# LSH attention, then a mixture of experts: first batch's x kept whole, its block sums in unit 4's first layer, the second batch's spread over units 5 to 7, attention's pace from 1300 to 2000

## The chip, the cores and the metric

The kernel runs on one core of a Trainium2 chip. The metric is the device time of one execution in microseconds (us); lower is better. The engines are TensorE (PE in the profile, with its weight loads as PEld), VectorE (DVE), ScalarE (ACT), GpSimd (POOL) and SyncE (SP), whose queue issues nearly all DMAs here.

## What is computed

```python
def _attn_ref(q, k, v, proj):        # q, k, v: 2 x 8 x 768 x 64; proj: 64 x 6
    q_bits = (np.einsum('bhsd,dk->bhsk', q, proj) > 0).astype(np.int64)
    ...
    mask = q_bucket[:, :, :, None] == k_bucket[:, :, None, :]
    scores = scale * np.matmul(q, k.transpose(0, 1, 3, 2))
    scores = np.where(mask, scores, -1000000000.0)
    scores = scores - np.max(scores, axis=-1, keepdims=True)
    attn = np.exp(scores)
    attn = attn / (np.sum(attn, axis=-1, keepdims=True) + 1e-09)
    return np.matmul(attn, v)

def _moe_ref(x, domain_probs, w1, w2):   # x: 1536 x 512; w1: 4 x 512 x 1024; w2: 4 x 1024 x 512
    p = domain_probs / (domain_probs.sum(-1, keepdims=True) + 1e-09)
    for e in range(E):
        h = np.maximum(x @ w1[e], 0.0)
        out += p[:, e:e + 1] * (h @ w2[e])
```

x is the attention's output, with the 8 heads side by side: 2 batches of 768 rows by 512 columns. All is float32.

## The kernel before

**Numbers.** A float32 product is made as three products of rounded parts: each operand is split into hi (ACT copies it into the rounded type) and lo (the operand minus hi, on POOL or DVE), and hi x hi, hi x lo and lo x hi are summed in PSUM.

**Attention.** Heads 0 to 7 belong to batch 0, heads 8 to 15 to batch 1. A head has six tiles of 128 rows. For each tile TensorE makes scores, DVE and ACT the exponentials. For heads 8 to 15 DVE turns blocks of 32 x 32 (`stage_x`, line 503, into `t`), three tiles to a group, and a DMA writes the group to DRAM (`scr`, line 509); four DMAs read it back in the wanted order into `pt` (`stage_y`, line 520). When both groups are there, TensorE makes the product with V in 24 matmuls (`stage_v`, line 538), DVE and ACT copy it out (`stage_u`, line 565), and POOL multiplies by the reciprocal of the row sums (`stage_m`). The pool `ptp` has three buffers for `pt`, `t` of the second group, and later for parts of w1. SP issues in order: the first reads of a head wait until the V product before has freed a buffer; then come the second group's write to `scr`, loads of the next head and of weights, and the second reads, which wait for that write to land.

For batch 0, `stage_m` writes x at once as hi and lo (tiles `xhi`, `xlo`), from a small tile `xf`, which then is free again. For batch 1 it leaves x whole in `xraw`.

**Experts.** The work on one batch is eight units (4 experts x 2 halves of 512 hidden columns), numbered 0 to 7 for batch 0 and 8 to 15 for batch 1. A unit is a first layer (x by w1, relu, split into `hh` and `hl`) and a second layer (by w2, six groups of rows, each added into `acc` by DVE, line 748). Units 0 to 4 are plain (`unit`): the first layer has eight groups of 12 matmuls of 384 columns. From unit 5 on (`FAST = 5`), `unit_fast` makes the first layer from seven products of blocks twice over instead of eight. These need sums of blocks of x, t1 = b12 - b11, t2 = b22 - t1, t4 = t2 - b21 and t3 = b22 - b12 (b11, b12 the left and right halves of x's first two row blocks, b21 and b22 of its last two), each split into hi and lo, and sums s1 to s4 of blocks of w1 (`split_w1_fast`). In the first product of a half, `pa` is copied out by ACT (`mt<-pa`, line 1060); the fourth product then adds into the same PSUM tile.

**Preparation before.** While a second layer runs, each of its six groups is followed by one step of the preparation of the next unit's w1. In unit 4's second layer the same groups are also followed by a step of `x_ops_first`: four adds on POOL rebuild x as hi + lo (line 882), and then each step makes one sum (DVE), its hi (ACT) and its lo (POOL or DVE). In unit 7's second layer the steps are those of `x_ops`, for batch 1: eight hi and lo pairs, five of them issued before the first group.

**Order.** The program is written out as one order by hand. Attention of batch 1 runs between the groups of batch 0's units: both are generators that yield their cost. After each yield of the experts (1960 for a first-layer group, 2600 for a second-layer group), the loop takes attention steps until their cost is level:

```python
n_att = sum(652 + ... for b, h, t in seq if b) + H * 1632 + (LAG_M[1] + 2) * DRAIN
...
    while da < dm * ATT_PACE * n_att / n_moe:
        x = next(att, None)
```

The steps after the last scores, in which the last heads are turned, read back and multiplied by V, cost `DRAIN` each. At the end of unit 4's first layer `drained()` issues what is left of attention.

Of the kernel before, what the change touches and what calls it, by code (L numbers as in the profile page):

```python
# [8 lines left out]
F32 = mybir.dt.float32  # L9
F32R = mybir.dt.float32r  # L10
ACTF = mybir.ActivationFunctionType
# [35 lines left out]
DRAIN = 1300  # L47
# [5 lines left out]
def tile_lsh_attention__then__domain_moe(  # L53
# [16 lines left out]
    KD = DM // P  # L70
    HALF = 512
# [20 lines left out]
    ptp = ctx.enter_context(tc.tile_pool(name="ptp", bufs=3))  # L92
# [8 lines left out]
    ps1 = ctx.enter_context(tc.tile_pool(name="ps1", bufs=4, space=PSUM))  # L101

# [300 lines left out]
    xf = {}  # L403
# [67 lines left out]
    def stage_t(b, h, t):  # L471
        pt, _ = probs_t.pop((b, h, t))
        g, o = divmod(t, G)
        if o == 0:
            if b or g == 0:
                t0 = ptp.tile([P, NT, GN], F32, tag="pt", name="pt")
                parts[b, h, g] = [t0[:, a : a + TW] for a in range(0, NT, TW)]
            else:
                parts[b, h, g] = [hp.tile([P, TW, GN], F32, tag=tag, name="pth") for tag in ("hh", "hl")]
            pts[b, h, g] = [x[:, c] for x in parts[b, h, g] for c in range(TW)]  # L480
        for i, a in enumerate(range(0, NT, TW)):
            ps = one("ptps")
            for c in range(TW):
                nc.tensor.transpose(ps[:, c * P : (c + 1) * P], pt[:, (a + c) * P : (a + c + 1) * P], ident)  # L484
            src = ps[:, : TW * P].rearrange("p (c n) -> p c n", c=TW)
            dst = parts[b, h, g][i][:, :, o * P : (o + 1) * P]
            if i and o % 2 == 0:
                nc.vector.tensor_copy(dst, src)
            else:
                nc.scalar.activation(dst, src, ACTF.Copy)  # L490
# [4 lines left out]
    def stage_x(b, h, t):  # L495
        g, o = divmod(t, G)
        if o == 0:
            pool, tag = (ptp, "pt") if g else (ex, "t1")
            turned[b, h, g] = pool.tile([P, G, S], F32, tag=tag, name="t1")
# [15 lines left out]
    def stage_y(b, h, g):  # L515
        scr = scrs.pop((b, h, g))
        pt = ptp.tile([P, NT, GN], F32, tag="pt", name="pt")
# [28 lines left out]

    def stage_u(b, h):
# [4 lines left out]
        for g in range(2):  # L552
            pts.pop((b, h, g))
            if b:
                x = xraw[:, j, g * GN : (g + 1) * GN]
            else:
                if not odd:
                    xf[b, j, g] = xs.tile([P, GN], F32, tag=f"xf{g}", name="xf", bufs=1)
                x = xf[b, j, g]
# [9 lines left out]
    def stage_m(b, h, g):  # L569
        j = h // 2  # L570
        sl = slice(g * GN, (g + 1) * GN)
        x = xraw[:, j, sl] if b else xf.pop((b, j, g))
# [166 lines left out]
    KH = KD // 2  # L739
# [18 lines left out]
    def second_layer(b, u, first_u, hs, w2, xo=None):  # L758
# [6 lines left out]
        for s in range(NS - 1, -1, -1) if blocks else range(NS):  # L765
            for t in range(TS):
# [23 lines left out]
                if xo is not None:  # L790
                    next(xo, 0)
# [3 lines left out]
        for _ in xo or ():  # L795
            pass
# [22 lines left out]
    def unit(b, u, first_u):  # L819
        w1hi, w1lo = wts[first_u + u, 0]  # L820
        sp2 = split_w(first_u + u, 1) if first_u + u else iter(())
        hs = {}
        for s in range(NS):
            sl = slice(s * SB, (s + 1) * SB)
            for f in range(FC):
# [14 lines left out]
                next(sp2, 0)  # L840
                yield 1960
# [31 lines left out]
    b11, b12 = xraw[:, 0:KH, 0:SB], xraw[:, 0:KH, SB:S]  # L873
    b21, b22 = xraw[:, KH:KD, 0:SB], xraw[:, KH:KD, SB:S]

    xrs = {}

    def x_ops_first():
        raw = ex.tile([P, 3, S], F32, tag="t1", name="xr")
        raws = [raw[:, j] for j in range(3)] + [ld.tile([P, S], F32, tag="tqk", name="xr3")]  # L880
# [4 lines left out]
        left, right = slice(0, SB), slice(SB, S)  # L885
        for n, j, sl in (("b11", 0, left), ("b21", KH, left), ("b22", KH, right)):
            xop[n] = tuple([x[0, j + kk][:, sl] for kk in range(KH)] for x in (xhi, xlo))
        pair_in("t1", ((xp, "xe0"),))
        pair_in("t2", ((xp, "xe1"),))
        t1 = combine(raw[:, 0:KH, right], raw[:, 0:KH, left], ALU.subtract)  # L890
        put_hi("t1", t1)
        put_lo("t1", t1, nc.gpsimd)
        yield

        def mixed_rows(f):
            t = pp.tile([P, KH, SB], F32, tag="p", name="xc")
# [12 lines left out]
        yield
        pair_in("t3", ((stk, "q1"), (stk, "al")))  # L910
        t3 = mixed_rows(lambda kk: dict(in0=raws[KH + kk][:, right], in1=raw[:, kk, right]))
        put_hi("t3", t3)
        put_lo("t3", t3, nc.vector)
        yield

    def x_ops():
        pair_in("b11", ((stk, "ah"), (stk, "k2")))
        pair_in("t1", ((stk, "ah"), (stk, "k2")))
        t1 = combine(b12, b11, ALU.subtract)
        put_hi("b11", b11)  # L920
# [12 lines left out]
        pair_in("b22", ((xp, "xe1"),))
# [80 lines left out]
    def unit_fast(b, u, first_u):  # L1014
# [151 lines left out]
```

## Time and profile before

| | |
|---|---|
| time, median of 3 runs (lowest to highest) | 733.28 us (730.88 to 734.75) |
| the profiled execution's own time | 732.77 us |
| its span | 730.7 us |
| PE busy | 709.9 us, 97% of the span |
| DVE busy | 512.3 us, 70% |
| ACT busy | 337.9 us, 46% |
| POOL busy | 319.6 us, 44% |
| granted clock, mean over the span | 0.988 |
| moved by DMA | 87.77 MB |

Busy is time in which an engine executes; the shares are means over stages with different limits. The granted clock is TensorE's, as a share of full speed. The span is what the profile covers, and 2.1 us of the execution's time lie outside it.

### The profile page before, as it was taken

What the parts mean: (1) busy time and instruction counts of PE and PEld (TensorE: products, weight loads), DVE (VectorE), ACT (ScalarE), POOL (GpSimd) and SP (SyncE); (2) the same over time, 40 slices, a digit from 0 to 9 for tenths busy, and PEclk for the clock granted to TensorE, in tenths of its full rate; (3) what the DMA queues carried; (4) which work ended last, traced back from release to release, by engine and by line L of the source; (5) the groups of instructions that cost most, each with busy time, mean ns of one, the idle gap of its engine ahead of it and who ended that gap; (6) DMA issues with size and microseconds to landing.
All of it is one profiled execution on the core that took longest, in us unless ns stands there. A gap on an engine that the chain in (4) does not pass through costs nothing.

```text
span 730.7 us, 10185 instructions
## 1 busy us (share of the span) xinstructions
PE 709.9 (97%) x3714; PEld 596.9 (82%) x3714; DVE 512.3 (70%) x806; ACT 337.9 (46%) x661; POOL 319.6 (44%) x289
## 2 busy tenths in 40 slices
PE   8999999999999999997979999899999999999998
PEld 6766766978878879875859989698988989899896
DVE  6898898858567657631597685987668576685863
ACT  6887887553553534512234343443434334353440
POOL 6358677524534534302654342753334242343420
PEclk9999999999999999998989999999999999999999
DMA  6323263988889869777011121142112221112202
GB/s 145 67 45 92 62 124 63 238 235 235 224 217 293 238 189 307 204 217 215 1 57 59 58 91 55 48 154 87 57 58 72 73 86 56 61 57 83 91 1 86
DMA packets 90849, 87.77 MB, mean 120 GB/s; under 512 B 53168, under 2 KB 55728, under 8 KB 90800
## 3 DMA queue, kind: packets, MB, share of 16 engines
q1 hardware_dynamic: 89776, 86.80, 42.8%
q8 instruction: 29, 0.48, 0.3%
q10 hardware_dynamic: 1024, 0.33, 0.2%
q14 instruction: 20, 0.16, 0.1%
HBM read 65.04 MB, written 22.07 MB: 119 GB/s over the span
## 4 chain that ended last, share of the span: by engine, by line
PE 79%; DVE 7%; DMA 6%; issue 3%; SPq 2%; POOL 1%; ACT 1%; POOLq 0%; DVEq 0%; ACTq 0%
PE mps L754 10%; PE mps L756 10%; PE mps L755 10%; PE pv L538 8%; DMA pt<-scr 3%; PE ptps L484 3%; PE sps L418 3%; PE sps L416 3%; PE mps L1026 3%; PE mps L1025 3%; PE mps L1022 3%; PE mps L801 3%; PE mps L803 3%; PE mps L802 3%; PE pa L1022 2%
## 5 line engine op out<-in xcount | busy, mean ns | idle before, releaser
L754 PE MATMUL mps<-w2hi,hh 128*128 128x512 f32 (+1 forms) x388 | 151.6, 391 | 3.2 <-DVE acc L748 3.2
L756 PE MATMUL mps<-w2hi,hl 128*128 128x512 f32 (+1 forms) x388 | 150.9, 389 | 0.0
L755 PE MATMUL mps<-w2lo,hh 128*128 128x512 f32 (+1 forms) x388 | 150.9, 389 | 0.0
L1008 POOL TENSOR_TENSOR w2lo<-ws,w2hi 128x512 fp32r<-128x512 f32 x44 | 56.0, 1297 | 145.6 <-ACT w2hi L1007 126.3
L423 DVE TENSOR_SCALAR_CACHE_REDUCE p<-sps 128x768 f32<-128x768 f32 x96 | 90.1, 940 | 20.9 <-PE sps L418 19.2
L748 DVE SCALAR_TENSOR_TENSOR acc<-mps,pe,acc 128x512 f32<-128x512 f32 (+1 forms) x85 | 62.9, 741 | 50.6 <-PE mps L756 49.4
L439 ACT ACTIVATE p<-p,nb 128x768 f32<-128x768 f32 x96 | 89.5, 932 | 18.7 <-DVE p L423 18.3
L754 PEld LDWEIGHTS mps<-w2hi,hh 128*128 128x128 f32 x388 | 73.2, 189 | 18.7 <-DVE acc L748 3.6
L756 PEld LDWEIGHTS mps<-w2hi,hl 128*128 128x128 f32 x388 | 73.2, 189 | 15.6
L755 PEld LDWEIGHTS mps<-w2lo,hh 128*128 128x128 f32 x388 | 73.3, 189 | 14.0
L538 PE MATMUL pv<-pt,tv 128*64 128x384 f32 x288 | 72.6, 516 | 4.8 <-DMA pt<-scr 4.7
L967 POOL TENSOR_TENSOR w1lo<-ws,w1hi 128x512 fp32r<-128x512 f32 x33 | 52.0, 1579 | 50.6 <-ACT w1hi L963 29.6
L1035 ACT ACTIVATE hh<-mt 128x384 fp32r<-128x384 f32 x66 | 34.7, 525 | 64.1 <-DVE mt L1080 40.8
L538 PEld LDWEIGHTS pv<-pt,tv 128*64 128x64 f32 x288 | 26.6, 143 | 40.7 <-issue 32.4
L835 ACT ACTIVATE hh<-mps 128x384 fp32r<-128x384 f32 x40 | 19.6, 489 | 79.7 <-PE mps L803 79.6
L503 DVE STREAM_TRANSPOSE t<-p 128x768 f32<-128x768 f32 x48 | 46.3, 964 | 12.1 <-ACT p L439 12.0
L416 PE MATMUL sps<-ah,q 128*128 128x384 f32 x192 | 53.9, 362 | 0.8 <-DVE p L423 0.8
L801 PE MATMUL mps<-xs,w1hi 128*128 128x384 f32 x160 | 54.1, 338 | 0.0
L803 PE MATMUL mps<-xs,w1lo 128*128 128x384 f32 x160 | 53.9, 337 | 0.0
L802 PE MATMUL mps<-xs,w1hi 128*128 128x384 f32 x160 | 53.8, 336 | 0.0
L233 POOL TENSOR_SCALAR q<-ah 64x768 fp32r<-64x768 f32 (+1 forms) x33 | 27.1, 822 | 59.2 <-ACT ah L345 44.9
L418 PE MATMUL sps<-k,al 76*128 76x384 f32 x192 | 49.9, 340 | 0.7 <-POOL k L233 0.3
(158 smaller groups left out, 1560.3 us busy)
## 6 DMA issues: line engine op xcount, KB each, us to landing
ws<-in_moe_w_dram SPq DMA_DIRECT2D x64, 512.0 KB, 3.9
scr<-t SPq DMA_DIRECT2D x16, 1152.0 KB, 8.5
pt<-scr SPq DMA_DIRECT2D x64, 288.0 KB, 6.0
tv<-in_v_dram SPq DMA_DIRECT2D x16, 192.0 KB, 5.2
tqk<-in_q_dram SPq DMA_DIRECT2D x30, 96.0 KB, 3.5
out_dram<-acc SPq DMA_DIRECT2D x11, 256.0 KB, 2.0
tqk<-in_k_dram SPq DMA_DIRECT2D x28, 96.0 KB, 3.5
rdb<-row SPq DMA_DIRECT2D x14, 192.0 KB, 6.1
```

What stands on the lines that cost most here:

```text
L416: nc.tensor.matmul(ps[:, i, :NH], q1[:, sl], k1[:, i * NH : (i + 1) * NH], start=True, stop=False)
L418: nc.tensor.matmul(ps[:, i, :NH], q2[0:MQE, sl], k2[0:MQE, i * NH : (i + 1) * NH], start=False, stop=True)
L423: nc.vector.tensor_scalar(out=two(pt), in0=ps[:, :, :NH], scalar1=MASKED, scalar2=MASKED, op0=ALU.min, op1=ALU.min, accum_out=nb,)
L439: nc.scalar.activation(pt, pt, ACTF.Exp, bias=nb, scale=-1.0, accum_out=dens[b, h, r][:, o : o + 1])
L538: nc.tensor.matmul(dst, vvs[b, h][:, c], pts[b, h, g][c], start=c == 0, stop=c == NT - 1, tile_position=(0, g * D),)
L748: nc.vector.scalar_tensor_tensor(out=acc, in0=ps, scalar=pcol, in1=acc, op0=ALU.mult, op1=ALU.add)
L754: nc.tensor.matmul(ps, hh[:, ts], w2hi[:, f, cs], start=n == 0, stop=False)
L755: nc.tensor.matmul(ps, hh[:, ts], w2lo[:, f, cs], start=False, stop=False)
L756: nc.tensor.matmul(ps, hl[:, ts], w2hi[:, f, cs], start=False, stop=n == FC - 1)
L801: nc.tensor.matmul(ps[:, :SB], w1hi[:, kk, fs], xhi[b, kk][:, sl], start=kk == 0, stop=False)
L802: nc.tensor.matmul(ps[:, :SB], w1hi[:, kk, fs], xlo[b, kk][:, sl], start=False, stop=False)
L803: nc.tensor.matmul(ps[:, :SB], w1lo[:, kk, fs], xhi[b, kk][:, sl], start=False, stop=kk == KD - 1)
```

## The change

The first batch's x is kept whole: `stage_u` and `stage_m` work in two tiles `xrs` (tags `xe0` and `xe1`) in place of the small `xf`, and the four adds that rebuilt x are gone. Its sums are made in unit 4's first layer, one step behind every other group of its eight; all lo parts are on POOL. They lie in the buffers of heads' q and k, so that they can stand only behind the last scores. For the second batch, `x_ops` is replaced by two generators: `x_ops_early` makes b11, t1 and t2 in unit 5's second layer and t4 and b21 in unit 6's, one step behind every other group, and `x_ops_late` makes b22 and t3 in unit 7's. `ptp` gets two buffers and a third under a tag of its own, which attention uses in the same turn of three as before. `DRAIN` goes from 1300 to 2000; the sum `n_att` of all attention costs thereby goes from 94080 to 102480.

```diff
-DRAIN = 1300
+DRAIN = 2000
...
-    ptp = ctx.enter_context(tc.tile_pool(name="ptp", bufs=3))
+    ptp = ctx.enter_context(tc.tile_pool(name="ptp", bufs=2))
...
+    def pt_tile(shape, name):
+        turn[0] += 1
+        if turn[0] % 3:
+            return ptp.tile(shape, F32, tag="pt", name=name)
+        return ptp.tile(shape, F32, tag="ptb", name=name, bufs=1)
...
-    xf = {}
+    xrs = [xp.tile([P, KH, S], F32, tag=f"xe{i}", name="xr") for i in range(KD // KH)]
...
+    def x_raw(b, j):
+        return xraw[:, j] if b else xrs[j // KH][:, j % KH]
...
-                if xo is not None:
+                if xo is not None and (nxt == NU or tt % 2):
                     next(xo, 0)
...
                 hs[s, f] = (hh, hl)
                 next(sp2, 0)
+                if first_u + u + 1 == FAST and f % 2:
+                    next(xo, 0)
                 yield 1960
...
-        xo = None
         if first_u + u + 1 == FAST:
             drained()
-            xo = x_ops_first()
-        yield from second_layer(b, u, first_u, hs, wts.pop((first_u + u, 1)), xo)
+        yield from second_layer(b, u, first_u, hs, wts.pop((first_u + u, 1)))
...
     def x_ops_first():
...
-        for j in range(KD):
-            nc.gpsimd.tensor_tensor(
-                out=raws[j], in0=xhi[0, j].bitcast(F32), in1=xlo[0, j].bitcast(F32), op=ALU.add
-            )
...
+        pair_in("t1", ((stk, "q1"), (stk, "al")))
         t1 = combine(b12, b11, ALU.subtract)
...
+        keep("t1", t1, nc.gpsimd)
+        yield
+        pair_in("t2", ((stk, "q1"), (stk, "al")))
         t2 = combine(b22, t1, ALU.subtract)
...
+        keep("t2", t2, nc.gpsimd)
+        yield
+        pair_in("t3", ((stk, "ah"), (stk, "k2")))
+        t4 = combine(t2, b21, ALU.subtract)
+        t3 = combine(b22, b12, ALU.subtract)
+        keep("t3", t3, nc.gpsimd)
+        yield
+        pair_in("t4", ((stk, "ah"), (stk, "k2")))
+        keep("t4", t4, nc.gpsimd)
+        yield
...
+    def x_ops_early():
...
+        pair("b11", xp, "xe0")
+        hi("b11", b11)
+        lo("b11", b11, nc.gpsimd)
+        yield
+        pair("t1", xp, "xe1")
+        t1 = combine(b12, b11, ALU.subtract)
+        hi("t1", t1)
+        lo("t1", t1, nc.gpsimd)
+        yield
+        pair("t2", ex, "t1")
+        t2 = combine(b22, t1, ALU.subtract)
+        hi("t2", t2)
+        lo("t2", t2, nc.gpsimd)
+        yield
+        pair("t4", ptp, "ptb", bufs=1)
+        t4 = combine(t2, b21, ALU.subtract)
+        hi("t4", t4)
+        lo("t4", t4, nc.gpsimd)
+        yield
...
+            nc.scalar.activation(h, b21[:, kk], ACTF.Copy)
+            nc.gpsimd.tensor_tensor(out=l, in0=b21[:, kk], in1=h.bitcast(F32), op=ALU.subtract)
+        yield
...
-        if first_u + u + 1 == NU:
-            xo = x_ops()
-            next(xo)
+        if not b:
+            xo = early if first_u + u + 1 < NU else x_ops_late()
         yield from second_layer(b, u, first_u, hs, wts.pop((first_u + u, 1)), xo)
+
+    early = x_ops_early()
```

The order of instructions changes at three places of interest. The first is DVE from the copy of head 14's result on (`xraw<-pv`), at the end of attention. `hl<-mps,hh` is the end of a first-layer group, `acc` that of a second-layer group, `wc` a sum of w1, `xc` a sum of x, `den` and `rd` the row sums of the last head. Before:

```order
L565 COPY xraw<-pv 64x4x3x32
L748 SCALAR_TENSOR_TENSOR acc<-mps,pe,acc 128x512
L450 TENSOR_SCALAR den<-den 128x6
L451 RECIPROCAL rd<-den 128x6
L836 SCALAR_TENSOR_TENSOR hl<-mps,hh 128x384 x6
L565 COPY xraw<-pv 64x4x3x32
L836 SCALAR_TENSOR_TENSOR hl<-mps,hh 128x384 x2
L748 SCALAR_TENSOR_TENSOR acc<-mps,pe,acc 128x512
L971 TENSOR_TENSOR wc<-ws 128x512
L971 TENSOR_TENSOR wc<-wc,ws 128x512
L870 TENSOR_TENSOR xc<-xr 128x768
L748 SCALAR_TENSOR_TENSOR acc<-mps,pe,acc 128x512
```

After:

```order
L572 COPY xraw<-pv 64x4x3x32
L754 SCALAR_TENSOR_TENSOR acc<-mps,pe,acc 128x512
L459 TENSOR_SCALAR den<-den 128x6
L460 RECIPROCAL rd<-den 128x6
L754 SCALAR_TENSOR_TENSOR acc<-mps,pe,acc 128x512 x3
L844 SCALAR_TENSOR_TENSOR hl<-mps,hh 128x384 x2
L878 TENSOR_TENSOR xc<-xr 128x768
L844 SCALAR_TENSOR_TENSOR hl<-mps,hh 128x384 x2
L878 TENSOR_TENSOR xc<-xr,xc 128x768
L844 SCALAR_TENSOR_TENSOR hl<-mps,hh 128x384
L572 COPY xraw<-pv 64x4x3x32
L844 SCALAR_TENSOR_TENSOR hl<-mps,hh 128x384
```

The first sum of x moved from behind both copies and the whole first layer of unit 4 to a place ahead of the last head's copy, and between the two copies stand four second-layer groups and five first-layer groups in place of one and six.

The second place is ACT in the second layer of unit 5, behind the last `hh` of its first layer; `w1hi` are the hi parts of unit 6's w1, `xo` those of x, and `mt<-pa` belongs to unit 6. Before:

```order
L1035 ACTIVATE hh<-mt 128x384 x3
L963 ACTIVATE w1hi<-ws 128x512 x2
L963 ACTIVATE w1hi<-wc 128x512 x2
L963 ACTIVATE w1hi_4002<-ws 128x512
L963 ACTIVATE w1hi_4002<-wc 128x512 x2
L1060 ACTIVATE mt<-pa 128x384
L1065 ACTIVATE mt<-pd 128x384
```

After:

```order
L1059 ACTIVATE hh<-mt 128x384 x3
L987 ACTIVATE w1hi<-ws 128x512 x2
L925 ACTIVATE xo<-xraw 128x768
L987 ACTIVATE w1hi<-wc 128x512 x2
L987 ACTIVATE w1hi_3989<-ws 128x512
L987 ACTIVATE w1hi_3989<-wc 128x512
L925 ACTIVATE xo<-xc 128x768
L987 ACTIVATE w1hi_3989<-wc 128x512
L925 ACTIVATE xo<-xc 128x768
L1084 ACTIVATE mt<-pa 128x384
L1089 ACTIVATE mt<-pd 128x384
```

Three copies for the second batch's x came in ahead of `mt<-pa`.

The third place is DVE in the second layer of unit 7, behind the last `hl` of its first layer. Before:

```order
L1040 SCALAR_TENSOR_TENSOR hl<-mt,hh 128x384
L870 TENSOR_TENSOR xc<-xraw 128x768
L870 TENSOR_TENSOR xc<-xraw,xc 128x768
L866 TENSOR_TENSOR xo<-xc,xo 128x768
L748 SCALAR_TENSOR_TENSOR acc<-mps,pe,acc 128x512
L971 TENSOR_TENSOR wc<-ws 128x512
L971 TENSOR_TENSOR wc<-wc,ws 128x512
L870 TENSOR_TENSOR xc<-xc,xraw 128x768
L748 SCALAR_TENSOR_TENSOR acc<-mps,pe,acc 128x512
```

After:

```order
L1064 SCALAR_TENSOR_TENSOR hl<-mt,hh 128x384
L754 SCALAR_TENSOR_TENSOR acc<-mps,pe,acc 128x512
L995 TENSOR_TENSOR wc<-ws 128x512
L995 TENSOR_TENSOR wc<-wc,ws 128x512
L754 SCALAR_TENSOR_TENSOR acc<-mps,pe,acc 128x512
L995 TENSOR_TENSOR wc<-ws 128x512
L995 TENSOR_TENSOR wc<-ws,wc 128x512
L878 TENSOR_TENSOR xc<-xraw 128x768
L754 SCALAR_TENSOR_TENSOR acc<-mps,pe,acc 128x512
```

Three instructions on x stood ahead of the first `acc` and one behind it; now one is left, behind the second `acc`.

## Rows read from the trace of the kernel before

**Rows 1.** TensorE's waits: operation, what it waited for, us, times, longest us

```profile
PE pv L538 <- DMA pt<-scr: 4.7, 2, 4.4
PE pa L1022 <- ACT mt L1060: 3.3, 1, 3.3
PE mps L754 <- DVE acc L748: 3.2, 1, 3.2
```

**Rows 2.** Stretches A:B; length; busy of each engine; granted clock, DMA share, GB/s

```profile
336.24:348.46 12.22, 7.86 (x26) 2.75 (x25) 0.56 (x1) 0.49 (x1) 1.51 (x2) 0.72 0.51 132
354.81:371.17 16.36, 16.36 (x74) 13.51 (x73) 13.83 (x10) 3.48 (x7) 14.10 (x7) 1.00 0.10 33
371.17:394.89 23.72, 18.46 (x85) 17.20 (x84) 18.65 (x27) 10.84 (x20) 9.46 (x7) 0.86 0.13 45
442.29:457.00 14.71, 14.71 (x86) 14.71 (x85) 8.64 (x15) 6.91 (x14) 4.42 (x4) 1.00 0.11 37
457.00:478.29 21.29, 18.14 (x73) 14.56 (x73) 19.59 (x18) 9.25 (x14) 15.77 (x8) 0.92 0.14 49
```

**Rows 3.** Chain that ended last: start us, duration us, what; attention's last heads

```profile
264.81 4.02 PE pv L538 x24
331.99 9.43 DMA pt<-scr
341.46 7.07 PE pv L538 x22
```

**Rows 4.** Timeline, POOL and ACT, units 4 and 5: start, us, instruction

```profile
357.34 8.88 POOL L882 TENSOR_TENSOR xr<-xs 128x768 f32<-128x768 f32 x4
380.49 0.84 ACT L862 ACTIVATE xo<-xc 128x768 fp32r<-128x768 f32 x1 [3.53 <-DVE xc L898]
381.24 0.47 ACT L1060 ACTIVATE mt<-pa 128x384 f32<-128x384 f32 x1
```

**Rows 5.** Timeline of DVE and POOL in unit 7's second layer

```profile
460.76 0.95 DVE L870 TENSOR_TENSOR xc<-xraw 128x768 f32<-128x768 f32 x1
461.75 2.49 DVE L870 TENSOR_TENSOR xc<-xraw,xc 128x768 f32<-128x768 f32 x1
461.07 2.35 POOL L866 TENSOR_TENSOR xo<-xraw,xo 128x768 fp32r<-128x768 f32 x1 [3.40 <-ACT xo L862]
```

**Rows 6.** Timeline of ACT in unit 6's first layer

```profile
412.55 0.49 ACT L1060 ACTIVATE mt<-pa 128x384 f32<-128x384 f32 x1 [7.65 <-PE pa L1026]
```

**Rows 7.** Stretches again, each between two products with V, heads 9 to 15

```profile
156.44:181.94 25.50, 25.50 (x128) 21.95 (x125) 17.96 (x30) 10.26 (x20) 8.74 (x8) 1.00 0.88 229
185.97:209.79 23.82, 23.82 (x126) 21.46 (x124) 17.97 (x30) 14.67 (x28) 13.33 (x13) 1.00 0.93 251
213.86:236.27 22.41, 21.97 (x114) 19.40 (x112) 13.95 (x25) 9.78 (x20) 7.74 (x7) 1.00 1.00 261
240.29:264.81 24.52, 24.52 (x127) 21.65 (x124) 18.45 (x30) 12.69 (x24) 12.15 (x12) 1.00 0.95 259
268.83:292.02 23.19, 23.19 (x127) 21.39 (x124) 15.14 (x27) 10.87 (x22) 7.76 (x7) 1.00 0.97 281
296.04:314.93 18.89, 18.89 (x93) 16.63 (x93) 13.03 (x23) 9.50 (x19) 7.56 (x6) 1.00 0.91 245
314.93:320.15 5.22, 4.84 (x26) 2.08 (x25) 1.64 (x2) 0.00 (x0) 0.00 (x0) 1.00 0.30 120
320.15:336.24 16.09, 16.09 (x85) 14.88 (x84) 4.56 (x9) 4.31 (x9) 3.51 (x3) 1.00 1.00 275
```

**Rows 8.** Tile pt on SP: second reads of head 11, then of head 13

```profile
L520 SPq DMA_DIRECT2D pt<-scr x4: 417/423/430, 226.5 to 227.9; - x4
DMA to landing us min/median/max: 5.7/6.9/8.0
...
L520 SPq DMA_DIRECT2D pt<-scr x4: 379/422/431, 280.6 to 282.0; - x4
DMA to landing us min/median/max: 4.5/6.0/6.7
```

More of the change, by code (lines that the diff above doesn't have):

```diff
@@ L70, in tile_lsh_attention__then__domain_moe @@
     KD = DM // P
+    KH = KD // 2
     HALF = 512
@@ L497, in stage_x @@
         if o == 0:
-            pool, tag = (ptp, "pt") if g else (ex, "t1")
-            turned[b, h, g] = pool.tile([P, G, S], F32, tag=tag, name="t1")
+            shape = [P, G, S]
+            turned[b, h, g] = pt_tile(shape, "t1") if g else ex.tile(shape, F32, tag="t1", name="t1")
         t1 = turned[b, h, g]
@@ L553, in stage_u @@
             pts.pop((b, h, g))
[L554 to L559, printed above, removed]
+            x = x_raw(b, j)[:, g * GN : (g + 1) * GN]
             dst, src = x[mine], ps[g * D : (g + 1) * D, :GN]
@@ L571, in stage_m @@
         sl = slice(g * GN, (g + 1) * GN)
-        x = xraw[:, j, sl] if b else xf.pop((b, j, g))
+        x = x_raw(b, j)[:, sl]
         if in_groups(b, h):
@@ L794, in second_layer @@
             pass
-        for _ in xo or ():
-            pass
+        if nxt == NU:
+            for _ in xo:
+                pass
     def first_layer(ps, w1hi, w1lo, b, f, sl, kks):
@@ L821, in unit @@
         sp2 = split_w(first_u + u, 1) if first_u + u else iter(())
+        xo = x_ops_first()
         hs = {}
@@ new lines, in tile_lsh_attention__then__domain_moe, with x_blocks, slices, keep @@
+    left, right = slice(0, SB), slice(SB, S)
+    def x_blocks(b):
+        top, low = (xraw[:, 0:KH], xraw[:, KH:KD]) if b else (xrs[0], xrs[1])
+        return top[:, :, left], top[:, :, right], low[:, :, left], low[:, :, right]
+    def slices(name, j, sl):
+        xop[name] = tuple([x[0, j + kk][:, sl] for kk in range(KH)] for x in (xhi, xlo))
+    def x_ops_first():
+        b11, b12, b21, b22 = x_blocks(0)
+        slices("b11", 0, left)
+        slices("b21", KH, left)
+        slices("b22", KH, right)
+        def keep(name, raw, eng):
+            put_hi(name, raw)
+            put_lo(name, raw, eng)
+        pair_in("t1", ((stk, "q1"), (stk, "al")))
+        t1 = combine(b12, b11, ALU.subtract)
+        keep("t1", t1, nc.gpsimd)
+        yield
+        pair_in("t2", ((stk, "q1"), (stk, "al")))
+        t2 = combine(b22, t1, ALU.subtract)
+        keep("t2", t2, nc.gpsimd)
@@ new lines, in x_ops_early, with pair, hi, lo @@
+    def x_ops_early():
+        def pair(name, pool, tag, **kw):
+            t = pool.tile([P, 2, KH, SB], F32R, tag=tag, name="xo", **kw)
+            next_ops[name] = (t[:, 0], t[:, 1])
+        def hi(name, src):
+            nc.scalar.activation(next_ops[name][0], src, ACTF.Copy)
+        def lo(name, src, eng):
+            h, l = next_ops[name]
+            eng.tensor_tensor(out=l, in0=src, in1=h.bitcast(F32), op=ALU.subtract)
+        b11, b12, b21, b22 = x_blocks(1)
+        pair("b11", xp, "xe0")
[3 more added lines that the diff above has]
+        pair("t1", xp, "xe1")
+        t1 = combine(b12, b11, ALU.subtract)
+        hi("t1", t1)
+        lo("t1", t1, nc.gpsimd)
+        yield
+        pair("t2", ex, "t1")
+        t2 = combine(b22, t1, ALU.subtract)
+        hi("t2", t2)
+        lo("t2", t2, nc.gpsimd)
@@ L934, in x_ops, with x_ops_late @@
+        yield
+    def x_ops_late():
+        xop.update(next_ops)
+        _, b12, _, b22 = x_blocks(1)
+        pair_in("b22", ((stk, "q1"), (stk, "al")))
         put_hi("b22", b22)
```

61 lines of the change are left out of this document (9 added, 52 removed).

## The prediction

> **What bounds the kernel now.** The first view is the page's busy line: TensorE is busy for 709.9 of the span's 730.7 us (the table of times). No other engine comes near, so a change can win only what TensorE loses by waiting, and by running at the lower clock after a wait. The second view is the list of TensorE's waits [rows 1]. The three that a change here can touch are 4.7 us for `pt<-scr` (probabilities that come back from DRAM turned), 3.3 us in the first products of unit 5 (for ACT's copy `mt<-pa`) and 3.2 us in the second layer of unit 7 (for `acc`).
>
> Waits alone understate the loss, so the third view is a table of stretches [rows 2]. A first layer in products takes 14.71 us when nothing is late (unit 7). In unit 5 it takes 23.72 us at a granted clock of 0.86. A second layer takes 16.36 us when clean (unit 4). In unit 7 it takes 21.29 us at 0.92. From the same rows come two unit prices: a second-layer group (B) is 16.36/6 = 2.73 us, and 14.71/84 x 12 = 2.10 us is 12 matmuls of 384 columns, as much as one plain first-layer group (A).
>
> The fourth view is the chain that ended last [rows 3]. A head's product with V takes 4.02 us undisturbed. The last head's begins 9.43 us after the last read of `scr` was issued, and its 22 remaining matmuls take 7.07 us. The window around it [rows 2] is 12.22 us, of which 7.86 are busy, at a mean granted clock of 0.72, so between the levels of 1.2 and 2.4 GHz. After 4.36 us idle it ran mostly on the low one.
>
> **Part 1: unit 5's operands.** Before, POOL first rebuilds x by four adds of 8.88 us together [rows 4]. The sums t1, t2, t4, t3 of x follow in unit 4's second layer, between the sums of w1 on DVE. The copy `mt<-pa`, needed before the fourth product, stands on ACT behind the last of the copies `xo<-xc`. It runs at 381.24 us, some 10 us after unit 5 began. After, x is kept whole, the four adds are gone, and the sums stand in unit 4's first layer, t1 and t2 ahead of the copy of the last head's result (first order fence). That is a whole second layer, 16.36 us, earlier. DVE's own share there is four sums of 0.95 us undisturbed [rows 5], beside TensorE's 2.10 us groups. All lo parts are now on POOL, four at 2.35 us or 9.4 us, beside the second half of a first layer and a whole second layer. Nothing there is wanted before unit 5. What is late next in unit 5 is w1's own preparation, and units 6 and 7 show that this alone is on time: their first layers are clean. Worth: 23.72 - 14.71 = 9.0 us.
>
> **Part 2: unit 7's second layer.** Before, five of eight operations for the second batch stand ahead of it, and the accumulation waits behind them on DVE: sums of 0.95 and 2.49 us and a lo part [rows 5]. TensorE, out of PSUM buffers, waits 3.2 us and then runs at the low clock. After, DVE has the accumulation first and one sum of x (third order fence). Worth: 21.29 - 16.36 = 4.9 us.
>
> **Part 3: what moves into units 5 and 6.** Five steps for the second batch now stand in their second layers, every other group. In unit 5 ACT gets three more copies (`xo`), all ahead of `mt<-pa` (second order fence). In unit 6's clean products that copy runs at 412.55 us with ACT idle for 7.65 us before it [rows 6]. Three copies of 0.84 us would fit into that, but they wait for sums and ACT is in order: w1's last sum, then t2, then its copy. By the durations of the two groups [rows 4, 5] the copy would be done 0 to 1 us after TensorE wants it. I take 0.5 us, with 0 and 3 us (a full POOL operation) as bounds. Unit 6's two steps have one sum of DVE and three copies of ACT, and I cost them at nothing. What covers them is the same 7.65 us, and their price without it would be in the same bounds.
>
> Here a rule speaks against the change. The trace shows a sum of x at 0.95 us where it began ahead of a POOL operation, and at 2.49 us where it began within one [rows 5]; the slow one ended 0.8 us after POOL's, as if it had waited for it. The Trainium skill, page "SBUF — State Buffer", section "SBUF: two separate sides", says that VectorE and GpSimd share a port pair as an exclusive lock, so that whichever starts first makes the other wait for the whole instruction. By that rule, and the trace agrees with its 2.49 us, a sum moved next to POOL's lo parts would pay up to one of them; the third rival gives the time.
>
> **Part 4: attention's pace and the close.** DRAIN enters the pace, so attention is issued 102480/94080 = 1.09 times as fast against the MoE groups, and its end lies earlier, with wider closing steps. Between two heads' V products stood 25.50, 23.82, 22.41, 24.52, 23.19, 18.89 and 16.09 us for heads 9 to 15 [rows 7]. The order of instructions shows other numbers of groups there: for head 9 5B+3A become 5B+1A (-4.2), then -1.3, -0.8, -1.9, -0.2, +0.2 and, for head 15, 2B+5A become 5B+3A (+4.0). The first order fence shows that last piece on DVE, where each `acc` row is a B group and each `hl` row an A group. So after: 21.3, 22.5, 21.6, 22.6, 23.0, 19.1 and 20.1 us, in sum 150.2.
>
> Against that stands a round trip. The first reads of a head wait for the V product before it to free `pt`; behind them on SP stands the second half's write to `scr`, behind that its reads, and V waits for these. From the end of the V product before to the last landing this took 227.9 + 8.0 - 213.86 = 22.0 us for head 11 and 282.0 + 6.7 - 268.83 = 19.9 us for head 13 [rows 7, 8], and 341.46 - 320.15 = 21.3 us for head 15 [rows 3, 7]. With 19.9 us for all, only head 14 waits, 0.8 us. With 22.0 us heads 9, 11, 14 and 15 wait 0.7 + 0.4 + 2.9 + 1.9 = 5.9 us. Heads 10, 12 and 13 have in the new order one more group ahead of their last transpose. If that delays their write by 2.1 to 2.7 us, another 5 us is possible. Bounds 0.8 and 11 us. I take 5.5, near the sum for 22.0 us: at 21.3 us it would be 2.2 + 1.2 = 3.4, and the late writes add something. Before, the last two heads lost 5.22 + 12.22 - 2 x 4.02 = 9.4 us. So this part is 5.5 - 9.4 = -3.9 us.
>
> **Sum.** The profiled execution took 732.77 us, 0.5 us under the median of 733.28 us. 732.77 - 9.0 - 4.9 + 0.5 - 3.9 = 715.5 us.
>
> **Rivals.**
> First, the round trip binds at every head. The mean of the three measured trips is 21.1 us. With one B group more each, 23.8 x 7 - 150.2 = 16.4 us of waiting in place of 5.5: 726.4 us. For it: the new order has the shortest gaps where they were longest. Against: only three heads have the later write.
>
> Second, on the slower side: each stalled head loses clock too. Head 15 before had 7.86 - 4.02 = 3.8 us more of busy time after its idle stretch. With a wait of 16.4/7 = 2.3 us a stalled head then costs 6.1 us. Everything else saves 9.0 + 4.9 + 9.4 - 0.5 = 22.8 us, so from four stalled heads on the change loses, and at seven it gives 732.77 - 22.8 + 42.7 = 752.7 us. For it: one row shows the price. Against: head 14 before was 0.38 us idle [rows 7] and kept a clock of 1.00, and the trips and gaps lie within 2 us of each other.
>
> Third, the preparation's waits only move into units 5 to 7. If each of the two units' moved sums pays a POOL operation (2.35 us), `mt<-pa` comes late by up to that, less a little slack: 4 us in all, 719.5 us.
>
> Fourth, the change doesn't do what it says at unit 5, since the sums wait behind late attention copies: nothing of the 9.0 us comes, 724.5 us. Against: the sums read the first batch's x, which is complete long before.
>
> **How the numbers follow.** Forecast 0.63; round trip 0.12; clock 0.06; moved waits 0.14; not done 0.05. A measurement of this kernel tells 0.5%, 3.7 us, from no change, so the bounds are 729.6 and 736.9 us. Faster: 0.62 of the forecast, 0.14, 0.05, and 0.07 of the round trip (its other part comes near the median): 0.88. Same: 0.06, from the round trip and one part of the forecast's edge. Slower: the clock, 0.06. Low end: 732.77 - 9.0 - 4.9 - 9.4 + 0.8 = 710.3, and a us for what the pace may save elsewhere. High end: 11 us of waits with 3 us of preparation, 723.5, and 3.8 us for one head that loses clock: 727 us.
>
> **What would show it.** Unit 5's first layer at 14.7 to 15.7 us with a clock near 1.00, and unit 7's second layer at 16.4 us, show parts 1 and 2 right. A wait for `mt<-pa` over 1 us in units 5 to 7 shows part 3 wrong. The waits for `pt<-scr` should be 1 to 11 us, spread over heads 9 to 15, none over 3 us; one of 4 us or more, with a clock near 0.7 in its window, would make part 4 and the sum wrong.

## Result, and the profile after

The changed kernel takes 714.13 us (median of 4 runs, 711.99 to 715.51) against 733.29 us before (4 runs, 730.88 to 734.75): a ratio of 0.9739, interval 0.9703 to 0.9775, or 19.2 us. The prediction said 715.5 us, with a low end of 710.3 us less about 1 us and a high end of 727 us.

The profiled execution of after is the fastest of its four, 711.99 us with a span of 710.3 us. The busy line of its profile page (engine, us, share of the span, instructions):

```profile
PE 701.6 (99%) x3714; PEld 593.3 (84%) x3714; DVE 502.7 (71%) x799; ACT 336.8 (47%) x662; POOL 317.6 (45%) x290
```

TensorE is at 99%, from 97%. Of the three waits of [rows 1], those for `mt<-pa` and `acc` are gone from its list; of those for `pt<-scr` one is left (operation, releaser, us, times, longest):

```profile
PE pv L547 <- DMA pt<-scr: 1.4, 1, 1.4
```

The table of stretches (A:B, length, busy of PE, PEld, DVE, ACT, POOL, granted clock, DMA share, GB/s) answers to [rows 2]: the first layers of units 5, 6 and 7, then unit 7's second layer.

```profile
364.52:379.24 14.72, 14.72 (x86) 14.72 (x85) 8.70 (x15) 6.90 (x14) 4.42 (x4) 1.00 0.11 36
395.59:410.69 15.10, 14.99 (x86) 14.67 (x84) 10.64 (x17) 7.53 (x15) 7.53 (x6) 1.00 0.13 37
427.02:441.74 14.72, 14.72 (x86) 14.72 (x85) 8.72 (x15) 6.90 (x14) 5.86 (x6) 1.00 0.11 39
441.74:458.09 16.35, 16.35 (x74) 13.51 (x73) 15.58 (x18) 6.59 (x11) 9.97 (x7) 1.00 0.33 112
```

Unit 5's first layer fell from 23.72 to 14.72 us and unit 7's second layer from 21.29 to 16.35 us, both at a clock of 1.00. Only unit 6's first layer is 0.4 us above its neighbours. The same view from the end of one product with V to the start of the next answers to [rows 7]; heads 9, 11, 14 and 15 are shown:

```profile
156.27:177.14 20.87, 20.87 (x100) 17.58 (x96) 15.68 (x26) 8.24 (x16) 6.70 (x7) 1.00 0.92 219
208.49:229.36 20.87, 20.87 (x100) 17.58 (x96) 15.32 (x26) 8.24 (x16) 6.71 (x7) 1.00 0.88 220
289.42:308.44 19.02, 19.02 (x105) 18.24 (x105) 13.19 (x24) 11.10 (x23) 6.39 (x6) 1.00 0.89 227
313.03:333.63 20.60, 20.60 (x99) 17.48 (x97) 6.56 (x11) 3.55 (x7) 3.83 (x3) 1.00 0.92 243
```

For heads 9 to 15 these stretches are 20.9, 23.1, 20.9, 23.1, 23.0, 19.0 and 20.6 us, where the prediction worked out 21.3, 22.5, 21.6, 22.6, 23.0, 19.1 and 20.1 us. Between heads 14 and 15 stand now 20.6 us in place of 16.1, and the last head no longer stalls.

### The profile page after: what moved, and what is told of

Same layout as the page of the kernel before. It is cut to its first block, busy times and chain, and to the rows that moved or that the text cites. A ratio compares the mean times of both kernels' runs of the same rounds, so it can differ in the third digit from the quotient of the medians.

```text
span 710.3 us, 10180 instructions
## 1 busy us (share of the span) xinstructions
PE 701.6 (99%) x3714; PEld 593.3 (84%) x3714; DVE 502.7 (71%) x799; ACT 336.8 (47%) x662; POOL 317.6 (45%) x290
## 4 chain that ended last, share of the span: by engine, by line
PE 88%; DVE 5%; POOL 2%; DMA 2%; issue 1%; ACT 1%; SPq 0%; POOLq 0%; DVEq 0%
PE mps L760 11%; PE mps L761 11%; PE mps L762 11%; PE pv L547 8%; PE mps L808 4%; PE mps L810 4%; PE mps L809 4%; PE sps L427 4%; PE sps L425 4%; PE ptps L493 4%; PE mps L1050 3%; PE mps L1049 3%; PE mps L1046 3%; PE pa L1046 2%; PE pa L1049 2%; PE pa L1050 2%
## 5 line engine op out<-in xcount | busy, mean ns | idle before, releaser
L547 PE MATMUL pv<-pt,tv 128*64 128x384 f32 x288 | 69.5, 492 | 1.7 <-DMA pt<-scr 1.4
```

The lines of the kernel that those rows point to most:

```text
L547: nc.tensor.matmul(dst, vvs[b, h][:, c], pts[b, h, g][c], start=c == 0, stop=c == NT - 1, tile_position=(0, g * D),)
```

## Experiments

Each of the twelve kernels was timed beside the kernel before. Ratios are to it, with their interval of 95%. The changed kernel's is 0.9739 (0.9703 to 0.9775).

### The pace apart from the rest

`after_d1300`:

```diff
-DRAIN = 2000
+DRAIN = 1300
```

> The changed kernel with DRAIN put back from 2000 to 1300 alone. TensorE's order of groups between the heads' products with V is then that of the kernel before (16 us of groups between heads 14 and 15), while the sums of x stay in unit 4's first layer. Theory (pace): the waits for pt<-scr at heads 14 and 15 and the low clock behind them come back, 5 to 8 us, so 719 to 722 us; units 5 and 7 stay clean (14.7 and 16.4 us). Rival (the stall had to do with the sums of x or the POOL adds, not with the pace): no such wait, 714 us. The round trip rival, had it been right, would make this kernel no slower.

Measured: 717.37 us, 0.9783 (0.9762 to 0.9804), 3.2 us more than the changed kernel; the two intervals still touch. TensorE's timeline at heads 14 and 15 (start, us, instruction, idle before it and its releaser):

```profile
317.53 4.05 PE L547 MATMUL pv<-pt,tv 128*64 128x384 f32 x22 [0.47 <-DMA pt<-scr]
341.68 4.08 PE L547 MATMUL pv<-pt,tv 128*64 128x384 f32 x22 [3.18 <-DMA pt<-scr]
```

The same rows of the changed kernel:

```profile
309.55 4.06 PE L547 MATMUL pv<-pt,tv 128*64 128x384 f32 x22 [0.25 <-issue]
333.63 4.09 PE L547 MATMUL pv<-pt,tv 128*64 128x384 f32 x24
```

The wait at the last head is back, 3.18 us, about as much as the difference. Not back is the low clock: the 22 matmuls behind the wait took 4.08 us, not the 7.07 us of [rows 3]. So the time is 1.6 us under the low end of what was expected.

`before_d2000` is the kernel before with

```diff
-DRAIN = 1300
+DRAIN = 2000
```

> The kernel before with DRAIN 2000 alone. Theory (pace): TensorE's order up to unit 4 is that of the changed kernel, so heads 14 and 15 no longer stall for long and 4 to 7 us are gained, 726 to 729 us; unit 5's first layer stays at 23 to 24 us and unit 7's second layer at 21 us. Rival: the pace only moves the stall into the other heads, 733 us.

Measured: 729.04 us, 0.9954 (0.9936 to 0.9972); 3.7 us below the 732.69 us of the kernel before, timed beside it. Its stretches of unit 5's first layer and unit 7's second layer:

```profile
368.46:392.88 24.42, 18.38 (x85) 17.23 (x84) 18.45 (x27) 10.82 (x20) 9.44 (x7) 0.79 0.13 43
454.98:476.35 21.37, 18.22 (x73) 14.59 (x73) 19.67 (x18) 9.25 (x14) 15.77 (x8) 0.92 0.16 49
```

Both keep their loss. DRAIN and the sums of x are thus two separate gains: 3.2 us with the sums moved, 3.7 us without.

### The two things that DRAIN does

DRAIN is the cost of a closing step and also a part of `n_att`, which sets the pace of all attention. Two runs take these apart, on the changed kernel.

`close_only`:

```diff
-ATT_PACE = 1.5
+ATT_PACE = 1.5 * 94080 / 102480
```

> The changed kernel with closing steps of 2000 but the pace of the kernel before (the factor divided by 1.09). By the order, the groups between V products are those of before for heads 9 to 13 (24.8, 23.5, 21.4, 24.1, 22.8 us by unit prices) and 21.3 and 19.3 us for heads 14 and 15. Theory (the wider closing steps do the work, the faster pace is a side effect): waits of 1 to 3 us, 713 to 715 us. Rival (the faster pace matters): 717 us like after_d1300.

`pace_only`:

```diff
-ATT_PACE = 1.5
+ATT_PACE = 1.5 * 102480 / 94080
...
-DRAIN = 2000
+DRAIN = 1300
```

> The changed kernel with the faster pace but closing steps of 1300. By the order 16.0 and 13.7 us of groups stand ahead of the products of heads 14 and 15, against a round trip of 20 to 22 us. Theory: waits of 4 to 6 and 6 to 8 us there, more than in the kernel before, perhaps with the low clock behind: 722 to 730 us. Rival (the faster pace is what helped): 714 us.

Measured: `close_only` 711.53 us, 0.9718 (0.9680 to 0.9756); `pace_only` 725.57 us, 0.9895 (0.9865 to 0.9925). With the two from above:

| | closing steps 1300 | closing steps 2000 |
|---|---|---|
| pace of before | 717.37 us | 711.53 us |
| pace times 1.09 | 725.57 us | 714.13 us |

The wider closing steps gain 5.8 us at the old pace and 11.4 us at the new one. The faster pace costs 8.2 us with narrow steps. With wide ones it seems to cost 2.6 us; there the intervals overlap, so the times alone don't separate `close_only` from the changed kernel. The trace supports it. Heads 14 and 15 of `close_only`:

```profile
317.83 4.09 PE L547 MATMUL pv<-pt,tv 128*64 128x384 f32 x24
341.50 4.34 PE L547 MATMUL pv<-pt,tv 128*64 128x384 f32 x24
```

No row of its waits names `pt<-scr`. Its second layer of unit 4 begins at 345.8 us; in the seven kernels of this study with the changed kernel's pace and closing steps and its order on SP (itself, `before_d2000` and the five further down that move sums, adds or steps) it begins at 348.2 to 352.1 us. The same two products of `pace_only`, and the stretch of the wait at the last head:

```profile
312.66 6.77 PE L547 MATMUL pv<-pt,tv 128*64 128x384 f32 x22 [3.43 <-DMA pt<-scr]
337.83 5.75 PE L547 MATMUL pv<-pt,tv 128*64 128x384 f32 x22 [3.79 <-DMA pt<-scr]
```

```profile
333.19:337.83 4.64, 0.86 (x3) 0.21 (x3) 0.75 (x1) 0.00 (x0) 0.00 (x0) 1.00 1.05 218
```

Waits of 3.43 and 3.79 us with a lower clock behind both: 22 matmuls took 6.77 and 5.75 us, at a granted clock of 0.59 and 0.70. During the wait the DMA share is 1.05, so the core's DMA engines are full while TensorE stands.

### What sets the round trip

`pace_less_read`, which leaves out a quarter of the read bytes and of the rows of the products, is `pace_only` with

```diff
-        for r in range(QD):
+        for r in range(QD - 1):
             nc.sync.dma_start(
...
-                    vvs[b, h][:, c],
-                    pts[b, h, g][c],
+                    vvs[b, h][:, c] if heavy(b, h, g * G) else vvs[b, h][:96, c],
+                    pts[b, h, g][c] if heavy(b, h, g * G) else pts[b, h, g][c][:96],
```

> The run pace_only with a quarter of the bytes of every read of scr left out (three of the four DMAs of a group; the products with V take 96 rows of the probabilities and V in place of 128, and the same columns and so about the same TensorE time; the result lacks that part). It asks what sets the round trip. Throughput: first reads, write and second reads are 1.18 MB each and go one after the other at some 270 GB/s, so 0.6 MB less is 2.2 us less per trip; the waits of 3.4 and 3.8 us fall to 1 to 2 us and the smaller ones go: 717 to 721 us. Latency (fixed times from issue to landing): waits and time stay, 724 to 726 us.

Measured: 714.85 us, 0.9747 (0.9719 to 0.9775), 10.7 us below `pace_only` and more than expected. The products of heads 14 and 15:

```profile
306.34 5.75 PE L547 MATMUL pv<-pt,tv 96*64 96x384 f32 x22 [1.65 <-DMA pt<-scr]
328.25 4.05 PE L547 MATMUL pv<-pt,tv 96*64 96x384 f32 x22 [1.52 <-DMA pt<-scr]
```

The writes to `scr` in the DMA view of `pace_only` (issue, queue, count, KB each, median us to landing), then of `pace_less_read`:

```profile
scr<-t SPq DMA_DIRECT2D x16, 1152.0 KB, 9.3
```

```profile
scr<-t SPq DMA_DIRECT2D x16, 1152.0 KB, 7.6
```

With a quarter of the reads gone the write also lands sooner, 7.6 us in place of 9.3, though it is as large as before. That speaks for throughput: the transfers share the engines. The waits fell by 1.8 and 2.3 us, near the 2.2 us worked out, but not by throughput alone: SP also issues one read less in each group. At the last head its timelines put some 0.9 of the 2.3 us on the fewer issues and 1.4 us on the write and the reads landing sooner. The rest of the gain of 10.7 us came from smaller waits and less time on the low clock.

`lag_y5` and `y0_5` tried to shorten the trip by SP's order.

```diff
-LAG_Y = 4
+LAG_Y = 5
```

> The changed kernel with the reads of pt (LAG_Y) one step later, so that on SP the second group's write to scr is issued ahead of the first group's reads, which wait for the V product before. Theory (the round trip begins at the V product before because the write queues behind those reads): the write starts up to 4 us earlier, the waits for pt<-scr fall to under 1 us, 711 to 713 us. Rival (the last transposes decide when the write can start): no change, 714 us, or slower if the reads come too late, 716 us.

Measured: 769.3 us, 1.0469 (1.0432 to 1.0505). It is 55 us above the changed kernel, where no change or a small one was expected. All its waits for `pt<-scr`, then head 10 in its timeline and stretches, and the landing of this head's second reads (tile pt on SP):

```profile
PE pv L547 <- DMA pt<-scr: 40.1, 7, 9.3
```

```profile
228.83 5.82 PE L547 MATMUL pv<-pt,tv 128*64 128x384 f32 x21 [8.69 <-DMA pt<-scr]
```

```profile
219.28:228.83 9.55, 0.86 (x4) 0.22 (x3) 1.88 (x4) 0.65 (x1) 3.75 (x4) 0.68 1.06 257
```

```profile
DMA to landing us min/median/max: 9.8/10.1/10.7
```

The order on SP tells why. In the changed kernel head 10's second reads stand ahead of the next head's first write (SP's timeline):

```profile
195.63 1.79 SPq L529 DMA_DIRECT2D pt<-scr  x4
198.25 0.38 SPq L518 DMA_DIRECT2D scr<-t  x1
```

In `lag_y5` the write stands ahead of the reads, and both then move at once:

```profile
213.65 0.38 SPq L518 DMA_DIRECT2D scr<-t  x1
214.13 0.46 SPq L708 DMA_DIRECT2D ws<-in_moe_w_dram  x1
214.68 3.77 SPq L529 DMA_DIRECT2D pt<-scr  x4
```

The reads landed 9.8 to 10.7 us after issue, where those of the same head in the changed kernel needed 4.5 to 6.7 us; DMA was at 1.06, and the product behind it ran mostly at the low clock (21 matmuls in 5.82 us). The later issue weighs more still: the last of these reads went out 21.2 us after the end of the product before, in place of 15.7 us. Of the 9.5 us that head 10's trip grew, 5.5 us are thus issue and 4.0 us landing.

`y0_5` moves only the first reads:

```diff
-LAG_Y = 4
+LAG_Y = (5, 4)
...
-                j = i - LAG_Y
-                if 0 <= j < n and j % G == G - 1 and not heavy(*seq[j]):
-                    b, h, t = seq[j]
-                    stage_y(b, h, t // G)
+                for g in range(NT // G):
+                    j = i - LAG_Y[g]
+                    if 0 <= j < n and j % NT == (g + 1) * G - 1 and not heavy(*seq[j]):
+                        b, h, t = seq[j]
+                        stage_y(b, h, g)
```

> The changed kernel with only the first group's reads of pt one step later (the second group's stay), so that SP issues the second group's write to scr ahead of the first group's reads and nothing else changes places much. If lag_y5 lost its time by the second reads (they were then issued a step later and behind the next head's write), this kernel has none of that loss. Theory (the write's queueing behind the first reads sets the round trip): waits for pt<-scr under 1 us, 711 to 713 us. Rival (the write starts by the last transposes, or the reads take the time it gains): 713 to 716 us. If instead the first reads themselves are what came late in lag_y5: over 730 us.

Measured: 727.57 us, 0.9928 (0.9905 to 0.9951), 13.4 us above the changed kernel. So some 42 of the 55 us did hang on the second reads, but the theory that the queueing of the write sets the trip fell. SP's timeline for head 10, TensorE's, and the stretch of the wait:

```profile
191.30 0.37 SPq L518 DMA_DIRECT2D scr<-t  x1
191.77 3.29 SPq L529 DMA_DIRECT2D pt<-scr  x4
213.68 5.27 PE L547 MATMUL pv<-pt,tv 128*64 128x384 f32 x21 [4.26 <-DMA pt<-scr]
```

```profile
208.50:213.60 5.10, 0.92 (x3) 0.19 (x2) 2.03 (x4) 2.37 (x4) 2.40 (x3) 0.98 1.05 273
```

SP waits at the write for the last transposes until 191.30 us, and the first reads, which could have gone out when the product before ended at 186 us, go behind it. Their four times 288 KB then move beside the write and the second reads, with DMA at 1.05. As the kernel had it, the reads use the time in which the write is not ready.

### The first batch's sums: the place and the four adds

| | label | in unit 4's first layer | in its second layer |
|---|---|---|---|
| without the adds | changed kernel, `sums_late` | 714.13 us | 716.51 us |
| with the adds | `adds_early`, `adds_late` | 713.82 us | 720.38 us |

`sums_late`:

```diff
-                if first_u + u + 1 == FAST and f % 2:
-                    next(xo, 0)
...
-                if xo is not None and (nxt == NU or tt % 2):
+                if xo is not None and (nxt in (FAST, NU) or tt % 2):
...
-        yield from second_layer(b, u, first_u, hs, wts.pop((first_u + u, 1)))
+        yield from second_layer(
+            b, u, first_u, hs, wts.pop((first_u + u, 1)), xo if first_u + u + 1 == FAST else None
+        )
```

> The changed kernel with the first batch's sums of x back in unit 4's second layer, one step behind each of its first four groups; x stays whole, so the four POOL adds stay out. Theory (place): the sums compete with those of w1 on DVE as before, unit 5's first layer is late again for most of its 9.0 us, 719 to 723 us. Rival (the adds were the cause): without the 8.9 us of adds the sums come in time and unit 5 stays near 14.7 us, 714 to 716 us.

`adds_early` (on the changed kernel) and `adds_late` (on `sums_late`) put this ahead of the sums:

```diff
+        for j in range(KD):
+            nc.gpsimd.tensor_tensor(
+                out=x_raw(0, j), in0=xhi[0, j].bitcast(F32), in1=xlo[0, j].bitcast(F32), op=ALU.add
+            )
```

> The changed kernel with the four POOL adds put back (x written again as hi + lo into the same tiles), ahead of the sums, in unit 4's first layer. Theory now (the adds cost only where the sums are late): at the early place a whole second layer hides their 8.9 us, unit 5's first layer stays at 14.7 us: 714 us. Rival (POOL has no room for 8.9 us more anywhere here): unit 5 is late by some us, 717 to 723 us.

> The run sums_late with the same four POOL adds ahead of the sums, so in unit 4's second layer as in the kernel before. Theory (adds and late place together make the 9.0 us): unit 5's first layer takes 20 to 24 us, 720 to 724 us. Rival (the 9.0 us came from the other differences to the kernel before, such as sums made in two halves and lo parts on DVE): unit 5 stays near 15.7 us, 716 to 717 us.

`junk_late` is `adds_late` with `out=junk[:, j % 3]`, a tile that nobody reads:

> The run sums_late with four POOL adds of the same shape, whose result goes to a tile that nobody reads, ahead of the sums. If POOL's time alone is what costs (its later lo parts start 8.9 us late, or its adds hold up DVE's sums), it comes out like adds_late, 720 to 724 us. If the sums' waiting for the rebuilt x is what costs, it stays near sums_late, 716 to 718 us.

Measured: `sums_late` 0.9775 (0.9747 to 0.9803), `adds_early` 0.9718 (0.9687 to 0.9749), `adds_late` 0.9810 (0.9781 to 0.9840), `junk_late` 721.44 us, 0.9833 (0.9791 to 0.9875). Unit 5's first layer in `sums_late`, `adds_late`, `junk_late` and `adds_early`, in this order:

```profile
366.24:381.92 15.68, 15.30 (x86) 14.54 (x84) 13.80 (x20) 8.90 (x17) 10.26 (x7) 1.00 0.21 67
```

```profile
365.53:387.46 21.93, 17.97 (x85) 17.28 (x84) 16.89 (x23) 10.62 (x20) 13.78 (x9) 0.84 0.15 48
```

```profile
367.89:388.39 20.50, 16.55 (x86) 15.86 (x84) 17.90 (x23) 10.63 (x20) 14.13 (x9) 0.92 0.16 51
```

```profile
366.99:381.70 14.71, 14.71 (x86) 14.71 (x84) 8.87 (x16) 6.90 (x14) 4.42 (x4) 1.00 0.15 53
```

The place alone costs 1.0 us of the stage, the adds at the early place nothing, and both together 7.2 us, with the clock at 0.84. So the theory in the expectation of `sums_late` was wrong, and its rival had the mechanism, though 716.51 us lies 0.5 us above the rival's range. And since `junk_late` loses nearly as `adds_late` does, what costs is POOL's time and not the waiting for a rebuilt x. How it reaches DVE is seen in the timelines, first of `sums_late`, then of `adds_late`:

```profile
354.22 0.69 DVE L995 TENSOR_TENSOR wc<-wc,ws 128x512 f32<-128x512 f32 x1
354.83 0.95 DVE L878 TENSOR_TENSOR xc<-xr 128x768 f32<-128x768 f32 x1
```

```profile
354.14 2.21 DVE L1000 TENSOR_TENSOR wc<-wc,ws 128x512 f32<-128x512 f32 x1
356.27 2.59 DVE L878 TENSOR_TENSOR xc<-xr 128x768 f32<-128x768 f32 x1
351.70 8.88 POOL L897 TENSOR_TENSOR xr<-xs 128x768 f32<-128x768 f32 x4
```

The same two instructions, the second sum of w1 and the first of x, take 0.69 and 0.95 us with POOL idle and 2.21 and 2.59 us within POOL's adds (2.22 and 2.59 us in `junk_late`). From there DVE has no pause, and each following step starts later, up to w1's last lo part on DVE, for which TensorE waits and then runs in part at the low clock (`adds_late`; `junk_late` has the same wait of 3.6 us):

```profile
PE mps L1055 <- DVE w1lo L996: 3.6, 1, 3.6
```

### The second batch's steps

`all_in_7`:

```diff
-            xo = early if first_u + u + 1 < NU else x_ops_late()
+            if first_u + u + 1 == NU:
+                xo = (x for g in (early, x_ops_late()) for x in g)
+                for _ in range(3):
+                    next(xo, 0)
```

> The changed kernel with all steps for the second batch back in unit 7's second layer, three of them (b11, t1, t2) ahead of its first group and one behind each of the next four. Theory: acc waits behind the sums on DVE, TensorE waits some 3 us and loses clock, unit 7's second layer takes 20 to 21.5 us in place of 16.4 us: 718 to 719 us. Rival (the steps spread over units 5 and 6 cost as much there): 714 us.

Measured: 721.32 us, 0.9840 (0.9820 to 0.9861), 7.2 us more than the changed kernel. Unit 7's second layer and unit 8's first, then two of TensorE's waits in the latter:

```profile
443.88:461.19 17.31, 16.63 (x74) 13.44 (x73) 16.52 (x15) 8.07 (x14) 12.13 (x7) 1.00 0.18 61
461.19:483.23 22.04, 18.49 (x85) 16.70 (x84) 14.31 (x22) 9.11 (x18) 15.47 (x11) 0.85 0.38 120
```

```profile
467.26 0.44 PE L1046 MATMUL pa<-xs,w1hi 128*128 128x384 f32 x1 [1.97 <-ACT mt L1084]
...
469.37 0.69 PE L1049 MATMUL pd<-xo,w1hi 128*128 128x384 f32 x1 [0.62 <-POOL xo L874]
```

The loss came, but at another place: only 1.0 us in unit 7's second layer, where it was expected, and 7.4 us in unit 8's first layer (22.04 us against 14.68 us of after): 3.55 us of idle time, and 18.49 us busy in place of 14.68 at a clock of 0.85. With three steps ahead and four behind, TensorE waits 0.7 us for `acc`, and the late lo parts on POOL and the late `mt<-pa` reach the next products.

## Why the prediction was right, point by point

**Part 1, 9.0 us: the size right, the reason half.** 23.72 - 14.72 = 9.0 us. The prediction named the adds that go and the move by a second layer, without saying which of them carries the 9.0 us. The runs show that either alone brings most of it, in kernels built on the changed one: leaving out the adds saves 21.93 - 15.68 = 6.2 us of the stage where the sums stand late, and moving the sums saves 21.93 - 14.71 = 7.2 us though the adds stay. What is left of the 9.0 us in the kernel before, some 2 us over `adds_late`, goes with the other differences of the sums there (made in halves, lo parts on DVE); no run took these apart.

**Part 2, 4.9 us: the size right, the reason not shown alone.** 21.29 - 16.35 = 4.9 us, and the wait for `acc` is gone. But `all_in_7`, which put the steps back, lost only 1.0 us in this layer and 7.4 us in the next. It has fewer steps ahead of the first group than the kernel before, and all its lo parts are on POOL, where one stood on DVE ahead of `acc`. So the runs show that the steps cost when they stand together late; which difference made them hold up `acc` in the kernel before stays open.

**Part 3, 0.5 us.** Measured 15.10 - 14.72 = 0.4 us, in unit 6, by the chain named: the sum for t2, its copy, then `mt<-pa`, then the fourth product. Timelines of DVE, POOL, ACT and PE of the changed kernel:

```profile
395.66 2.04 DVE L878 TENSOR_TENSOR xc<-xraw,xc 128x768 f32<-128x768 f32 x1
395.15 1.73 POOL L991 TENSOR_TENSOR w1lo<-wc,w1hi 128x512 fp32r<-128x512 f32 x1
397.73 0.85 ACT L925 ACTIVATE xo<-xc 128x768 fp32r<-128x768 f32 x1 [4.13 <-DVE xc L878]
398.48 0.47 ACT L1084 ACTIVATE mt<-pa 128x384 f32<-128x384 f32 x1
399.00 0.45 PE L1046 MATMUL pa<-xs,w1hi 128*128 128x384 f32 x1
```

The sum takes 2.04 us and not 0.95, with a POOL operation begun 0.5 us before it, and ends 0.8 us after that one; the copy ends at 398.95 us and the product begins at 399.00 us, where without the wait it would begin at 398.73 us, 0.17 us behind the matmul before it. The third rival, moved waits of 4 us, didn't come: its mechanism is here, but it bit once and with slack ahead of it. The page "SBUF — State Buffer" of the Trainium skill, section "SBUF: two separate sides", which the prediction weighed, says that the port pair shared by VectorE and GpSimd goes to whichever starts first for its whole instruction, while the other is blocked. This row and the 2.59 us above agree: a sum begun within a POOL operation takes more than twice its time alone.

**Part 4, -3.9 us: the size near, its inside wrong.** By medians the whole of DRAIN is worth 3.2 us (with the sums moved) to 3.7 us (without). The profiled executions show more. From the end of head 8's product to unit 5 the kernel before took 371.17 - 156.44 = 214.7 us and after 364.52 - 156.27 = 208.3 us, 6.5 us less. But after's is the fastest run. In it TensorE stood 1.7 us at products with V (1.4 us for `pt<-scr`), in the profiles of the six others of its pace, closing steps and order on SP 1.9 to 5.0 us, where 5.5 us were forecast.

Two steps inside the term were wrong. First, the prediction took the faster pace and the wider closing steps as one. They work against each other: the closing steps alone make the gain, and the pace shortens the stretches between products, which brings the waits that are left. Second, it gave all heads a trip of nearly 22.0 us. Head 11's second reads in the changed kernel:

```profile
L529 SPq DMA_DIRECT2D pt<-scr x4: 406/423/439, 221.0 to 222.4; - x4
DMA to landing us min/median/max: 7.4/8.5/9.2
```

By the prediction's own working its trip was 222.4 + 9.2 - 208.49 = 23.1 us; that of head 14 was 20.1 us and that of head 15 18.9 us. So the 2.9 and 1.9 us of waiting that the 22.0 us gave heads 14 and 15 shrank to 0.25 us and nothing, and head 11's 0.4 us grew to 1.4 us. No wait came of the late writes of heads 10, 12 and 13 in this profile. So the term is right only as a sum: the heads on which it laid its waits are not those that waited, and that part is luck.

**The sum.** In the two profiled executions the parts come to 9.0 + 4.9 - 0.4 + 6.5 = 20.0 of 20.8 us. Half a us more is unit 8's first layer, which the prediction did not name: 478.29 to 493.48 us before, so 15.19 us, and 458.09 to 472.77 us after, so 14.68 us.

**Rivals.** That the trip binds at every head, and that the clock falls at each stalled one, didn't happen in the changed kernel, but `lag_y5` comes near both: it has 40.1 us of waits in seven products, with 21 or 22 matmuls taking 5.4 to 6.5 us behind six of them, and a clock of 0.68 in the stretch shown. The last rival (sums behind late attention copies) didn't come: unit 5's first layer is clean.

**A faster version.** `close_only`, at 711.53 us and with no wait for `pt<-scr`, is the fastest measured. Against the kernel before it is clear; against the changed kernel its 2.6 us stand on the trace and not on the intervals.

## What to carry to other kernels

A number that stands for a cost in a pacing sum does two things when it is changed; make both changes apart before keeping them. Long GpSimd operations cost here though nobody read their result (`junk_late`), because two-input sums of VectorE ran beside them: put such work where the next deadline is far, or leave it out. The write to DRAM that is read back was slowed by the bytes in flight beside it, so look at the DMA share while the consumer waits before the queue's order is changed.

## What the runs showed of the hardware that was not expected

The length of an idle stretch did not tell whether TensorE came back at its low clock. After 3.18 us idle (`after_d1300`) 22 matmuls took 4.08 us at a granted clock of 1.00, so at the 2.4 GHz level. After 3.43 us (`pace_only`) they took 6.77 us at 0.59, so mostly at the 1.2 GHz level; after 1.65 us (`pace_less_read`) 5.75 us at 0.70, and after 1.52 us in the same kernel 4.05 us at 1.00. The price of 3.8 us that the second rival took from one row was therefore one draw of several.
